# Attention spread evenly over the MLP, and a third MLP pair by seven products, on one Trainium2 core

## The chip, the cores and the metric

The kernel runs on one core of one Trainium2 chip. A time is the device time of one execution in microseconds, and a kernel's time is the median of several executions. A profile is one execution taken by the hardware profiler. The engines are named as the profile names them: PE (TensorE matmuls), PEld (TensorE weight loads), DVE (VectorE), ACT (ScalarE), POOL (GpSimd) and SP (SyncE, which here only issues DMAs).

## The reference

There are 8 batches, 12 heads, 448 positions, 64 values a head, so a model width of 768, and a hidden width of 3072. All inputs and the output are float32.

```python
q_n, k_n = rmsnorm(q, g_q), rmsnorm(k, g_k)            # over the 64 values of a head
attn = softmax(q_n @ k_n.T / sqrt(64))                  # 448 x 448, per batch and head
x    = heads_side_by_side(attn @ v)                     # (8, 448, 768)
h    = x.transpose(0, 2, 1) @ U @ V                     # mixes positions, rank 32
u    = x + h.transpose(0, 2, 1)
out  = u + relu(u @ w_ch1) @ w_ch2                      # 768 -> 3072 -> 768
```

## The kernel before

The 8 x 448 positions are cut into 28 tiles of 128 rows; two batches make seven tiles, so that the middle tile of seven holds the end of one batch and the start of the next. The kernel has two kinds of work. Attention makes x for one batch at a time; the MLP takes u in tiles. After a hand-written head (batch 0's attention), the MLP runs as a chain of generators: the first three tiles, a single tile, and then twelve pairs of tiles, `mlp_pair(g)` for g = 1 to 12 with tiles 2g+2 and 2g+3. Each `yield` in a generator is a step of some six matmuls. All engines take their instructions in the order in which the program issues them (`tc.manual_schedule`), and no scheduler moves them.

**A pair.** `mlp_pair` has two layers, called ph and po here after their PSUM tiles. In the first layer of an ordinary pair (L638 to L652), each of 24 blocks of hidden values takes 6 matmuls of 256 columns (L643), 144 in all, and one relu serves two blocks (L428 on ACT, L430 on DVE). The second layer uses a Strassen-Winograd form: 7 products of 12 matmuls of 384 columns, 84 in all (L519), with sums of weights (T1 to T4) and of hidden values (S1 to S4, L527). The products are called W, Z, X and Y by their banks; W, X and Y get two products each, Z one. DVE adds x (L674, L677, L696), and the rest goes through `part` (L686, L699, L711); POOL does two of the additions (L687, L702). At the end of it `put` stores the two tiles.

**A late pair.** From pair `LATE` = 11 on, the first layer goes through `products_late`, the same scheme for `w_ch1`: 7 products of 36 matmuls of 128 columns (L592), 252 in all, in an order written out as "10 50 11 20 ..." (product, then third of the hidden width). Three groups (72, 32 and 42) are held back into the second layer. It needs four sums of weights with 12 pieces each, R1, R2, R4 and R3, where R3 takes the place of V21 inside `w1b`, and four sums of u (`sums_u`). Copies on ACT (L602, L604) and additions on DVE (L606, L608) carry partial results between PSUM and two buffers, `held`, which live in the buffers E of attention. In the first late pair alone, two dummy matmuls (L601) write two banks once.

**Queues within the program.** `later` puts small sums into `pending`, `spread` puts the sums of weights into `slack`. Each `step` first issues one of `pending` or, if there is none, one of `slack`; then it lets the MLP take a step. A late pair first empties `slack`.

**Weaving.** `weave(fill, upto, items)` spreads the pieces of a batch's attention (or of its mixing, `mixing`) evenly over MLP steps up to a place. `attention(b)` makes pairs of heads p = 6b to 6b+5: scores (L303), exps (L311), value products (L318) and their normalization (L333 to L347) into x; along the way squares (L235), reductions (L240), `rsqrt` (L245, L246), scalings (L255) and gains (L290) for pairs of heads two to four ahead, and their loads. Where three scores come in one session, one of them uses two banks of the pool "mm" (tile `sh`), which the MLP and the value products use too: it has four. R1 is put into `slack` at pair of heads 44, R2 and R4 at 46, into buffers that attention has just done with. The places where attention ends:

```python
ends = {2: ("po", 1), 3: ("po", 3), 4: ("ph", 5), 5: ("po", 6), 6: ("po", 8), 7: ("po", 10)}
for b, key in ends.items():
    weave(fill, place(key, 0.05), attention(b))
    weave(fill, place(key, 0.6), mixing(b))
```

Counted in stages (a stage is a pair, its first layer the first 0.533 of it), attention 2 ends at 1.557, 3 at 3.557, 4 at 5.027, 5 at 6.557, 6 at 8.557 and 7 at 10.557, each mixing some 0.257 later.

**Rings.** x has NX = 9 places, u has 4. `have_read` tells that a pair has read its u, and issues the transposes on SP that waited for the place (`turn_u`, L405). With nine places some normalizations of three tiles wrap around the ring and are split into two instructions (L342). `sums` and `rms` have six slots of 16, by pair of heads.

Of the kernel before, what the change touches and what calls it, by code (L numbers as in the profile page):

```python
# [10 lines left out]
FP32 = mybir.dt.float32  # L11
BF16 = mybir.dt.bfloat16
# [6 lines left out]
def kernel(  # L19
# [74 lines left out]
    one = consts.tile([1, 1], FP32, name="one")  # L94
    eps = consts.tile([SP, 1], FP32, name="eps")
    rk0 = consts.tile([SP, 8], FP32, name="rk0")
    sums = consts.tile([SP, 6 * 16], FP32, name="sums")
    NE, NV, NQ, NWARM = 2, 3, 4, 12
    Ew = [consts.tile([P, 2, PAD + NJ * S + PAD], BF16, name=f"E{i}") for i in range(NE)]
    Es = [e[0:SP] for e in Ew]  # L100
    vw = [consts.tile([P, HG, NJ, D + 1], BF16, name=f"va{i}") for i in range(NV)]
    vas = [v[0:SP] for v in vw]


    NX, NU = 9, 4
    xr = consts.tile([P, NX, dm], BF16, name="xr")
    ur = consts.tile([P, KD, NU * P], BF16, name="ur")
    zero = xr[:, NX - 1]
# [2 lines left out]
    vL = consts.tile([P, HG, NJ * D], FP32, name="vt")  # L111
    part = consts.tile([P, HALF], FP32, name="part")

    rms = consts.tile([SP, 6 * 16], FP32, name="rms")
    banks0 = []

    def rs_of(p, n=1, of=None):

        c = 16 * (p % 6)
        return (of or (banks0[3][0:SP] if p < 8 and p not in (2,) else rms))[:, c:c + 16 * n]  # L120

    def as_v(x):
# [9 lines left out]
    def setup():  # L132
        nc.vector.memset(zero, 0.0)
        nc.gpsimd.memset(eps, D * 1e-6)
        nc.gpsimd.memset(one, 1.0)
        for i, g in enumerate((g_q, g_k)):
            nc.gpsimd.dma_start(grow[:, i], bass.AP(g.tensor, g.offset, [[0, 1], [0, 2], [1, D]]))
        nc.gpsimd.memset(shift, 0.0)
        make_identity(nc, ident)
        for t in Es:  # L140
            nc.gpsimd.memset(t[:, :, 0:PAD], 0.0)
            nc.gpsimd.memset(t[:, :, PAD + NJ * S:], 0.0)
        for t in vas:
            nc.gpsimd.memset(t[:, :, :, D:D + 1], 1.0)
        for t in qkTs:
            nc.gpsimd.memset(t[:, SQK:], 0.0)
        nc.gpsimd.memset(Vsh, 0.0)
# [157 lines left out]
            scs[p, kc] = sc  # L305

    def expo(p, kc):
        E, sc = Es[p % NE][:, :, PAD + kc * S:PAD + (kc + 1) * S], scs.pop((p, kc))
        parts = [(E, sc[2][0:SP, :, 0:S])] if len(sc) > 2 else [(E[:, h], sc[h][0:SP, 0:S]) for h in range(2)]
        for dst, src in parts:  # L310
            nc.scalar.activation(dst, src, AF.Exp, scale=float(D) ** 0.5)  # L311

    def products(p, hh, o):
        par, E, va, hl = p // 6 % 2, Es[p % NE], vas[(p // 2) % NV], 2 * (p % 2) + hh
        for i, off in enumerate(OFFS[par]):
            for kc in range(NJ):
                c = PAD + kc * S + off
                nc.tensor.matmul(o[:, i, :], E[:, hh, c:c + P], va[:, hl, kc, :],  # L318
                                 start=(kc == 0), stop=(kc == NJ - 1))

    def tiles_of(b):
# [85 lines left out]
    def have_read(ts):  # L407
        read.update(ts)
        for t in [t for t in waiting if t - NU in read]:
            waiting.remove(t)  # L410
            turn_u(t)
# [14 lines left out]
    def relu(out, ph, on_act):  # L426
        if on_act:
            nc.scalar.activation(out, ph, AF.Relu)  # L428
        else:
            nc.vector.tensor_relu(out, ph)  # L430
# [5 lines left out]
    def put(t, osb, cols=slice(0, dm), engines=(nc.sync, nc.sync)):  # L436
        b, off = where(t)
        if off < 0:
            store(b - 1, 384, 448, osb, 0, cols, engines)
            store(b, 0, 64, osb, 64, cols, engines)  # L440
        else:
            store(b, off, off + P, osb, 0, cols, engines)
# [83 lines left out]
    def later(fn, *args):  # L526
        pending.append(lambda: fn(*args))  # L527

    LATE = 11
    wq = w1b.rearrange("p (d i) (k j n) -> p j d k i n", d=2, j=2, n=P)  # L530
    Q = KH // 2
    V11, V12, V21, V22 = ([wq[:, j, d, k] for k in range(Q)] for j in range(2) for d in range(2))
    R1, R2, R4 = [], [], []
    R3 = V21
    tq = Ew[0][:, 0, 0:4 * KD // 2 * P].rearrange("p (c i n) -> p c i n", c=4, n=P)
    flat = Ew[1].rearrange("p a n -> p (a n)")
    held = [x.bitcast(FP32) for x in (Ew[0][:, 1, 0:1024], flat[:, 0:1024], flat[:, 1024:2048], flat[:, 2048:3072])]

    def pieces(tile_, names, dtype=FP32):
        x = tile_.rearrange(names)  # L540
# [30 lines left out]
    def products_late(g, u):  # L571
        b11, b21, b22 = quarter(u, 0, 0), quarter(u, 1, 0), quarter(u, 1, 1)
        t1, t2, t3, t4 = (tq[:, c] for c in range(4))
        sides = {1: (V11, b11), 2: (V12, b21), 3: (R4, b22), 4: (V22, t4), 5: (R1, t1), 6: (R2, t2), 7: (R3, t3)}
        Pb, Zb, Qb = {}, {}, {}

        def bank(tag):
            if tag == "s":
                return ps_s.tile([P, 2, 512], FP32, tag="s", name="sc")[:, 0]
            return ps_mm.tile([P, 512], FP32, tag="mm", name="ph")  # L580

        def one(m, n):
            ks = slice(4 * n, 4 * n + 4)
            left, right = sides[m]
            if m == 1:
                Pb[n] = bank("mm")
            elif m == 5:
                Zb[n] = bank("mm")
            to = {1: Pb, 2: Pb, 5: Zb, 3: Zb}.get(m, Qb)[n]
            for j in range(4):  # L590
                for i in range(KD // 2):
                    nc.tensor.matmul(to[:, j * P:(j + 1) * P], left[4 * n + j][:, i], right[:, i],  # L592
                                     start=m in (1, 5) and j == 0 and i == 0, stop=i == KD // 2 - 1,
                                     skip_group_check=True)
                if j % 2:
                    yield 2 * P
            keep, tmp = held[n % 2], held[2 + n % 2]
            if m == 1:
                Qb[n] = bank("s")
                if g == LATE and n < 2:  # L600
                    nc.tensor.matmul(Qb[n], w1b[:, 0, 0:P], w1b[:, 0, 0:512], start=True, stop=True)  # L601
                nc.scalar.copy(Qb[n], Pb[n])  # L602
            elif m == 5:
                nc.scalar.copy(keep, Zb[n])  # L604
            elif m == 6:
                nc.vector.tensor_tensor(Zb[n], Qb[n], keep, OP.add)  # L606
            elif m == 7:
                nc.vector.tensor_tensor(tmp, Qb[n], keep, OP.add)  # L608
                relu(hB[:, 3, ks].rearrange("p k n -> p (k n)"), tmp, True)
            elif m == 2:  # L610
                relu(hB[:, 0, ks].rearrange("p k n -> p (k n)"), Pb.pop(n), True)
            elif m == 3:
                relu(hB[:, 1, ks].rearrange("p k n -> p (k n)"), Zb.pop(n), False)
            else:
                relu(hB[:, 2, ks].rearrange("p k n -> p (k n)"), Qb.pop(n), True)
                sums_h(n)

        def run(order):
            for word in order.split():
                yield from one(int(word[0]), int(word[1]))  # L620

        yield from run("10 50 11 20 60 51 21 70 30 61 40 12 52 71 31 22 62 41")
        return run("72 32"), run("42")
# [7 lines left out]
    def mlp_pair(g):  # L631
        t0, u, last = 2 * g + 2, u_of(2 * g + 2, 2), 2 * g + 4 == 28
        left = None
        if g >= LATE:
            while slack:
                slack.pop(0)()
            left = yield from products_late(g, u)
        for k in range(KH // 2 if g < LATE else 0):  # L638
# [13 lines left out]
            yield 2 * P  # L652
        if g == LATE - 1:
            spread(nc.vector.tensor_tensor, R3, V11, V21, OP.subtract)
        have_read([t0, t0 + 1])
        x0, x1 = x_of(t0), x_of(t0 + 1)
        c0, c1 = slice(0, HALF), slice(HALF, dm)
        osb0, osb1 = new_osb(), new_osb()
# [5 lines left out]
        for n in product(W, A11, B11, True):  # L664
            yield n
            if left:
                yield from left[0]
        nc.scalar.copy(part, W)
        yield HALF
        if left:  # L670
# [26 lines left out]
            yield c.stop - c.start  # L697
        yield from product(X, S3, T3, False)
        nc.vector.tensor_tensor(part, X, part, OP.add)  # L699
        if not last:  # L700
            both = osb1.rearrange("p (h n) -> p h n", h=2)
            nc.gpsimd.tensor_tensor(both, both, part.rearrange("p n -> p () n").to_broadcast([P, 2, HALF]), OP.add)  # L702
            put(t0 + 1, osb1)
# [102 lines left out]
    def step(fill):  # L806
        if pending:
            pending.pop(0)()
        elif slack:
            slack.pop(0)()  # L810
        n = next(fill, None)
        if n is not None:
            at[0] += n
        return n

    def weave(fill, upto, items):
        weights, total = sum(w for w, _ in items), upto - at[0]
        done = due = 0.0
        for w, piece in items:
            due += w * total / max(weights, 1)  # L820
            while done < due:
                n = step(fill)
                if n is None:
                    break
                done += n
            piece()
# [163 lines left out]
    with tc.manual_schedule():  # L990
# [32 lines left out]
        def place(key, share):  # L1023
            return begins[key][0] + share * begins[key][1]
# [24 lines left out]
        load(8)  # L1049
        while at[0] < place("single", 0):  # L1050
            step(fill)
        ends = {2: ("po", 1), 3: ("po", 3), 4: ("ph", 5), 5: ("po", 6), 6: ("po", 8), 7: ("po", 10)}
        for b, key in ends.items():
            weave(fill, place(key, 0.05), attention(b))
            weave(fill, place(key, 0.6), mixing(b))
        while step(fill) is not None:
            pass

# [29 lines left out]
```

## Time and profile before

| | us |
|---|---|
| median of 3 runs | 563.0 (562.41 to 564.17) |
| the profiled execution | 561.54 |
| its span, first to last instruction | 559.8 |
| pairs 1 to 10, from 122.1 to 497.7 | 36.3 to 40.6 each |
| pair 11 (497.7 to 527.5) | 29.8 |
| pair 12 with the end (527.5 to 559.8) | 32.3 |

The profiled execution's time is 1.7 us more than its span, for what lies around the first and last instruction. The granted TensorE clock is 1.00 in the whole span. A row of the profile's waits reads "engine tile line <- releaser: us in total, times, longest". In the chain, a piece is its start, its length and what ran. Busy times of matmuls overlap each other, so that a rate is read from the steps of the chain and not from the mean of a row.

### The profile page before, as it was taken

What the parts mean: (1) busy time and instruction counts of PE and PEld (TensorE: products, weight loads), DVE (VectorE), ACT (ScalarE), POOL (GpSimd) and SP (SyncE); (2) the same over time, 40 slices, a digit from 0 to 9 for tenths busy, and PEclk for the clock granted to TensorE, in tenths of its full rate; (3) what the DMA queues carried; (4) which work ended last, traced back from release to release, by engine and by line L of the source; (5) the groups of instructions that cost most, each with busy time, mean ns of one, the idle gap of its engine ahead of it and who ended that gap; (6) DMA issues with size and microseconds to landing.
All of it is one profiled execution on the core that took longest, in us unless ns stands there. A gap on an engine that the chain in (4) does not pass through costs nothing.

```text
span 559.8 us, 13728 instructions
## 1 busy us (share of the span) xinstructions
PE 549.7 (98%) x5688; PEld 387.3 (69%) x5690; DVE 366.0 (65%) x827; ACT 316.7 (57%) x536; POOL 177.7 (32%) x174
## 2 busy tenths in 40 slices
PE   8999999999999999999999999999999999989996
PEld 3665565767768677586785785776867758768785
DVE  6977867498655656656566677465464585785554
ACT  7967640778357574487548780765717746315150
POOL 6964026444051340344404440433205320010200
PEclk9999999999999999999999999999999999999999
DMA  8999996945555551365347565635605121040101
GB/s 287 292 235 239 204 251 182 201 144 160 130 112 135 146 141 64 75 186 147 90 142 160 134 145 116 155 85 153 170 16 126 42 19 59 2 114 1 52 7 56
DMA packets 108445, 72.41 MB, mean 129 GB/s; under 512 B 56688, under 2 KB 105056, under 8 KB 108384
## 3 DMA queue, kind: packets, MB, share of 16 engines
q1 hardware_dynamic: 96800, 61.65, 43.8%
q0 software_dynamic: 11008, 9.44, 10.4%
q8 instruction: 44, 0.72, 0.5%
q10 hardware_dynamic: 576, 0.46, 0.3%
q14 instruction: 17, 0.14, 0.1%
HBM read 56.78 MB, written 11.01 MB: 121 GB/s over the span
## 4 chain that ended last, share of the span: by engine, by line
PE 91%; ACT 5%; DVE 3%; issue 1%
PE po L519 30%; PE ph L643 28%; PE o L318 8%; PE sc L303 4%; PE po L474 4%; PE ph L456 3%; ACT E L311 3%; PE ph L592 3%; PE sh L303 3%; PE sc L592 2%; PE px L395 1%; PE sc L830 1%; DVE comb L515 1%; PE ph L484 1%; PE sc L843 1%
## 5 line engine op out<-in xcount | busy, mean ns | idle before, releaser
L643 PE MATMUL ph<-ur,w1b 128*128 128x256 bf16 x1440 | 170.9, 273 | 0.0
L643 PEld LDWEIGHTS <-w1b 128*128 128x128 bf16 x1440 | 135.7, 98 | 26.2 <-issue 10.0
L519 PEld LDWEIGHTS <-hT 128*128 128x128 bf16 x1032 | 96.2, 98 | 64.7 <-issue 7.7
L311 ACT ACTIVATE E<-sc 112x896 bf16<-112x896 f32 x138 | 121.8, 918 | 2.1 <-PE sc L303 2.1
L255 POOL TENSOR_TENSOR qkn<-qk,rms 112x512 bf16<-112x512 f32 (+1 forms) x73 | 80.8, 1127 | 109.0 <-ACT rms L246 96.4
L519 PE MATMUL po<-w2b,hT 128*128 128x384 bf16 (+1 forms) x588 | 103.8, 323 | 0.2 <-ACT hT L428 0.2
L311 ACT ACTIVATE E<-sh 112x448 bf16<-112x448 f32 x108 | 52.9, 541 | 90.1 <-PE sh L303 90.1
L428 ACT ACTIVATE hT<-ph 128x512 bf16<-128x512 f32 (+1 forms) x110 | 64.3, 587 | 52.1 <-PE ph L643 45.0
L527 DVE TENSOR_TENSOR hT<-hT 128x512 bf16<-128x512 bf16 x144 | 71.6, 508 | 12.9 <-ACT hT L428 10.8
L519 PE MATMUL po<-comb,hT 128*128 128x384 bf16 (+1 forms) x444 | 78.3, 322 | 0.0
L687 POOL TENSOR_TENSOR osb<-osb,xr 128x384 f32<-128x384 f32 x12 | 12.8, 1071 | 187.5 <-DVE osb L686 181.2
L318 PEld LDWEIGHTS <-E 112*128 112x128 bf16 x1536 | 60.7, 98 | 8.8 <-issue 2.8
L318 PE MATMUL o<-va,E 112*128 112x65 bf16 x1344 | 57.1, 194 | 0.1
L333 DVE RECIPROCAL rec<-o 128x4 f32<-128x4 f32 x84 | 15.0, 179 | 55.3 <-PE o L318 54.9
L430 DVE TENSOR_SCALAR hT<-ph 128x512 bf16<-128x512 f32 (+1 forms) x48 | 31.8, 662 | 29.3 <-PE ph L643 27.0
L240 DVE TENSOR_REDUCE sums<-sq 112x16 f32<-112x1024 f32 x32 | 38.7, 1210 | 6.4 <-ACT sq L235 6.3
L303 PE MATMUL sc<-qkT 64*128 64x448 bf16 x268 | 38.9, 351 | 1.0 <-ACT E L311 0.6
L474 PE MATMUL po<-w2b,hT 128*128 128x384 bf16 x192 | 34.5, 326 | 0.1
L235 ACT ACTIVATE sq<-qk 112x1024 f32<-112x1024 f32 x32 | 33.8, 1056 | 0.0
L342 DVE TENSOR_TENSOR xr<-o,rec 128x192 bf16<-128x192 f32 (+1 forms) x108 | 31.5, 310 | 2.9
L397 DVE TENSOR_TENSOR xr<-px,xr 128x384 bf16<-128x384 f32 x56 | 29.5, 549 | 5.4 <-PE px L393 2.9
L303 PEld LDWEIGHTS <-qkT 64*128 64x128 bf16 x376 | 14.3, 94 | 25.6 <-issue 15.8
(153 smaller groups left out, 566.0 us busy)
## 6 DMA issues: line engine op xcount, KB each, us to landing
qk<-in_q_dram SPq DMA_DIRECT2D x44, 256.0 KB, 4.3
qk<-in_k_dram SPq DMA_DIRECT2D x44, 256.0 KB, 4.9
vt<-in_v_dram SPq DMA_DIRECT2D x17, 512.0 KB, 6.2
w1b<-in_moe_w_ch_dram POOLq DMA_DIRECT2D x6, 768.0 KB, 19.5
w2b<-in_moe_w_ch_dram POOLq DMA_DIRECT2D x6, 768.0 KB, 36.5
comb<-in_v_dram SPq DMA_DIRECT2D x5, 512.0 KB, 8.8
out_dram<-osb SPq DMA_DIRECT2D x7, 336.0 KB, 3.2
out_dram<-osb SPq DMA_DIRECT2D x7, 288.0 KB, 3.1
```

The costliest lines, as they stand in the source:

```text
L235: nc.scalar.activation(dst, src, AF.Square)
L240: nc.vector.tensor_reduce(rs_of(p, of=sums).rearrange("p (s h j) -> p s h j", s=2, h=2)[:, :, hs], sqs[p].rearrange("p (s h j d) -> p s h ...
L255: (nc.gpsimd if p >= 12 or pool else nc.vector).tensor_tensor(out[:, g], x[:, g], rs[:, g].to_broadcast([SP, g.stop - g.start, NJ, D]), OP ...
L303: nc.tensor.matmul(sc[hh][0:n, 0:S], flat[pp, c:c + n], blocks(p)[pp, :, 0], start=True, stop=True)
L311: nc.scalar.activation(dst, src, AF.Exp, scale=float(D) ** 0.5)
L318: nc.tensor.matmul(o[:, i, :], E[:, hh, c:c + P], va[:, hl, kc, :], start=(kc == 0), stop=(kc == NJ - 1))
L428: nc.scalar.activation(out, ph, AF.Relu)
L430: nc.vector.tensor_relu(out, ph)
L474: nc.tensor.matmul(po, left(hc), w2b[:, half, hc, :], start=(hc == 0), stop=(hc == KH - 1))
L519: nc.tensor.matmul(bank, left[:, k, :], right[:, k, cols], start=start and k == 0, stop=k == KH // 2 - 1, skip_group_check=not start)
L527: pending.append(lambda: fn(*args))
L643: nc.tensor.matmul(out, w1b[:, dc, hc * P:(hc + 1) * P], u[:, dc, :], start=(dc == 0), stop=(dc == KD - 1))
```

## The change

- `LATE` becomes 10, so the first layer of pair 10 goes through seven products too. `have_read` of a late pair comes after the groups that are held back, since they read u.
- Attention of batch b ends at stage 1.557 + 1.6 (b - 2), its mixing 0.257 later: 1.557, 3.157, 4.757, 6.357, 7.957 and 9.557.
- A step without `pending` issues two of `slack`. A late pair first issues all of `pending`, then `slack` down to the 12 sums of R3; each group of product 7 issues the R3 that it reads, if they are still there.
- In pairs 9, 10 and 11 DVE makes the last two additions to `osb1` (two instructions) in place of POOL (one).
- x has 10 places; `sums` and `rms` have four slots. The two halves of E share the padding between them. `held` is two buffers, and product 7 adds in place.

```diff
-    sums = consts.tile([SP, 6 * 16], FP32, name="sums")
+    sums = consts.tile([SP, 4 * 16], FP32, name="sums")
...
-    Ew = [consts.tile([P, 2, PAD + NJ * S + PAD], BF16, name=f"E{i}") for i in range(NE)]
+    ROW = NJ * S + PAD
+    Ew = [consts.tile([P, PAD + 2 * ROW], BF16, name=f"E{i}") for i in range(NE)]
...
-    NX, NU = 9, 4
+    NX, NU = 10, 4
...
-        c = 16 * (p % 6)
+        c = 16 * (p % 4)
...
-    LATE = 11
+    LATE = 10
...
-    held = [x.bitcast(FP32) for x in (Ew[0][:, 1, 0:1024], flat[:, 0:1024], flat[:, 1024:2048], flat[:, 2048:3072])]
+    held = [Ew[1][:, i * 1024:(i + 1) * 1024].bitcast(FP32) for i in range(2)]
...
+            while m == 7 and len(slack) > Q - 4 * (n + 1):
+                slack.pop(0)()
...
-                nc.vector.tensor_tensor(tmp, Qb[n], keep, OP.add)
-                relu(hB[:, 3, ks].rearrange("p k n -> p (k n)"), tmp, True)
+                nc.vector.tensor_tensor(keep, Qb[n], keep, OP.add)
+                relu(hB[:, 3, ks].rearrange("p k n -> p (k n)"), keep, True)
...
         if g >= LATE:
-            while slack:
+            while pending:
+                pending.pop(0)()
+            while len(slack) > Q:
                 slack.pop(0)()
...
-        have_read([t0, t0 + 1])
+        if not left:
+            have_read([t0, t0 + 1])
...
             if left:
                 yield from left[0]
+                have_read([t0, t0 + 1])
...
-        if not last:
+        if LATE - 1 <= g and not last:
+            for h in (c0, c1):
+                nc.vector.tensor_tensor(osb1[:, h], osb1[:, h], part, OP.add)
+            put(t0 + 1, osb1)
+        elif not last:
...
     def step(fill):
         if pending:
             pending.pop(0)()
-        elif slack:
-            slack.pop(0)()
+        else:
+            for _ in slack[:2]:
+                slack.pop(0)()
...
-        ends = {2: ("po", 1), 3: ("po", 3), 4: ("ph", 5), 5: ("po", 6), 6: ("po", 8), 7: ("po", 10)}
-        for b, key in ends.items():
-            weave(fill, place(key, 0.05), attention(b))
-            weave(fill, place(key, 0.6), mixing(b))
+        def stage(x):
+            g = int(x)
+            return begins["ph", g][0] + (x - g) * (begins["ph", g + 1][0] - begins["ph", g][0])
+
+        for b in range(2, B):
+            end = 1.557 + 1.6 * (b - 2)
+            weave(fill, stage(end), attention(b))
+            weave(fill, stage(end + 0.257), mixing(b))
```

More of the change, by code (lines that the diff above doesn't have):

```diff
@@ L112 @@
     part = consts.tile([P, HALF], FP32, name="part")
-    rms = consts.tile([SP, 6 * 16], FP32, name="rms")
+    rms = consts.tile([SP, 4 * 16], FP32, name="rms")
     banks0 = []
     def rs_of(p, n=1, of=None):
-        c = 16 * (p % 6)
+        c = 16 * (p % 4)
         return (of or (banks0[3][0:SP] if p < 8 and p not in (2,) else rms))[:, c:c + 16 * n]
@@ L140, in setup @@
         for t in Es:
-            nc.gpsimd.memset(t[:, :, 0:PAD], 0.0)
-            nc.gpsimd.memset(t[:, :, PAD + NJ * S:], 0.0)
+            nc.gpsimd.memset(t[:, 0:PAD], 0.0)
+            nc.gpsimd.memset(t[:, PAD:].rearrange("p (h n) -> p h n", h=2)[:, :, NJ * S:], 0.0)
         for t in vas:
@@ L307, in expo @@
     def expo(p, kc):
-        E, sc = Es[p % NE][:, :, PAD + kc * S:PAD + (kc + 1) * S], scs.pop((p, kc))
+        E = Es[p % NE][:, PAD:].rearrange("p (h n) -> p h n", h=2)[:, :, kc * S:(kc + 1) * S]
+        sc = scs.pop((p, kc))
         parts = [(E, sc[2][0:SP, :, 0:S])] if len(sc) > 2 else [(E[:, h], sc[h][0:SP, 0:S]) for h in range(2)]
@@ L316, in products @@
             for kc in range(NJ):
-                c = PAD + kc * S + off
-                nc.tensor.matmul(o[:, i, :], E[:, hh, c:c + P], va[:, hl, kc, :],
+                c = PAD + hh * ROW + kc * S + off
+                nc.tensor.matmul(o[:, i, :], E[:, c:c + P], va[:, hl, kc, :],
                                  start=(kc == 0), stop=(kc == NJ - 1))
@@ L534 @@
     R3 = V21
-    tq = Ew[0][:, 0, 0:4 * KD // 2 * P].rearrange("p (c i n) -> p c i n", c=4, n=P)
-    flat = Ew[1].rearrange("p a n -> p (a n)")
-    held = [x.bitcast(FP32) for x in (Ew[0][:, 1, 0:1024], flat[:, 0:1024], flat[:, 1024:2048], flat[:, 2048:3072])]
+    tq = Ew[0][:, 0:4 * KD // 2 * P].rearrange("p (c i n) -> p c i n", c=4, n=P)
+    held = [Ew[1][:, i * 1024:(i + 1) * 1024].bitcast(FP32) for i in range(2)]
     def pieces(tile_, names, dtype=FP32):
@@ L596, in one @@
                     yield 2 * P
-            keep, tmp = held[n % 2], held[2 + n % 2]
+            keep = held[n % 2]
             if m == 1:
```

## The prediction, as it was put on record

> **What bounds the kernel now.** I read the page first: engine shares, then the chain that ended last, then what TensorE waited for, the chain in order of time and the stretches by stage.
>
> ```profile
> PE 549.7 (98%) x5688; PEld 387.3 (69%) x5690; DVE 366.0 (65%) x827; ACT 316.7 (57%) x536; POOL 177.7 (32%) x174
> ...
> PE 91%; ACT 5%; DVE 3%; issue 1%
> ```
>
> TensorE is the bound: 91% of the chain, and it is busy in 98% of the span. Since a busy matmul row may still be waiting, I looked at what TensorE waited for by name (in total, times, longest):
>
> ```profile
> PE sc L601 <- DVE w1b L547: 1.5, 1, 1.5
> PE sc L830 <- DVE xr L133: 1.3, 1, 1.3
> PE sh L303 <- ACT hT L428: 1.0, 2, 0.6
> PE sc L303 <- ACT E L311: 0.6, 2, 0.4
> PE sc L303 <- DVE qkT L274: 0.3, 1, 0.3
> PE po L519 <- ACT hT L428: 0.2, 1, 0.2
> ```
>
> Five of these six lie before 145 us, where the change moves nothing on TensorE, or at 500 us (L601). Between 145 and 497 us the one wait is the last row, 0.23 us at 295.5 us. So there are two things to win: matmul columns, and the wait at L601. The pieces of the chain that price them (start us, us, what), from an ordinary pair's first layer and from the seven-product one:
>
> ```profile
> 404.34 3.93 PE ph L643 x36
> ...
> 497.88 0.68 PE ph L592 x12
> 498.57 0.04 issue
> 498.61 0.55 DVE osb L711
> 499.15 0.27 DVE qkn L547
> 499.42 0.55 DVE w1b L547 x2
> 499.96 0.04 issue
> 500.01 0.38 PE sc L601
> 500.38 1.34 PE ph L592 x24
> ```
>
> A 256-column step takes 3.93/36 = 109.2 ns, a 128-column one 1.34/24 = 55.8 ns, and the chain leaves TensorE for VectorE just once late in the kernel, at 498.6 us.
>
> **A third pair by seven products.** Pair 10's first layer was 144 x 109.2 ns = 15.72 us. It becomes 7 x 36 = 252 matmuls x 55.8 ns = 14.06 us. The gain is 1.66 us of pure TensorE time. The trace holds the result already: pair 12 runs its first 216 late matmuls in 12.0 us (527.5 to 539.5), at 55.6 ns, with no wait. The two 512-column dummies (L601) only move from pair 11 to pair 10. ScalarE gets 6 copies and loses 3 relus, VectorE gets 3 relus, 6 additions of 0.69 us and 4 sums of u: ScalarE was busy 7.1 of 12.0 us and VectorE 6.1 in that stage of pair 12, so TensorE hides them.
>
> [...]
>
> **The weight sums.** In the old order the 12 sums R3 come last in VectorE's queue and the first L601 reads two of them, so TensorE stood from 498.34 to 500.01 us, 1.67 us for a 0.05 us step: 1.62 us. Ahead of them stood one sum of 1.98 us where its neighbours start 0.27 us apart:
>
> ```profile
> 496.66 1.81 POOL L702 TENSOR_TENSOR osb<-osb,part 128x768 f32<-128x768 f32 x1 [3.50 <-DVE part L699]
> 496.71 1.98 DVE L547 TENSOR_TENSOR qkn<-w1b,qkn 128x384 bf16<-128x384 bf16 x1
> ```
>
> This is GpSimd's addition at L702 holding VectorE up. In pairs 9 to 11 it becomes two VectorE additions (0.55 us each by L707): 1.1 us more work, but GpSimd has only L687 left there.
>
> In the new order R1 (12 sums) is issued in pair 8's second layer, R2 and R4 (24) in pair 9's first, and six of R3 among the first 30 matmuls of pair 9's second; the first L601 then finds its two R3 long done and waits for nothing. What is late next? Behind product X, VectorE has part (0.56), two additions (1.10), one sum of u (0.35), two R3 (0.54) and L711 (0.55), 3.1 us in all. From X's end TensorE has 12 x 0.163 = 1.95 us of Y, then 48 narrow matmuls, 2.7 us, before the group that needs L711's bank: 4.6 us of cover. So the 1.62 us goes, and VectorE may be 1.5 us late before anything comes back.
>
> Is VectorE that late? Counted in the order of the changed program, each instruction at its row's mean, it has in pair 9 19.0 us beside some 20.2 us of TensorE in the first layer and 18.4 beside 16.1 in the second; for pair 10 before, the same count gives 16.1 and 20.7, of which the trace shows 11.6 and 14.1 us busy, because neighbouring instructions overlap, and TensorE waited nowhere ahead of L601. New is that two sums a step are popped: up to ten in 3.3 us of TensorE, 10 x 0.27 = 2.7 us where GpSimd is idle, which fits. I take zero; the bounds are 0 (a wait cannot be negative) and the whole 1.62 us.
>
> **Attention at even distances.** Matmul count and work are the same; only the places move. Batch 3 shrinks from 1.74 stages to 1.34, batches 6 and 7 likewise; batches 4 and 5 stretch from 1.21 and 1.27 to 1.34. The old wait of 0.23 us sits at batch 5's start and goes with it. New waits come if ScalarE falls behind: by the same count, the new first layer of pair 7 holds 21.0 us of ScalarE beside 20.3 of TensorE, those of pairs 2, 4 and 5 19.2 to 19.5. But pair 4 before held 22.2 beside 21.4, without a wait.
>
> ```profile
> core 0: us, PE busy (x) PEld busy (x) DVE busy (x) ACT busy (x) POOL busy (x), PEclk, DMA share, GB/s
> 122.10:145.40 23.30, 23.08 (x280) 18.24 (x279) 19.53 (x48) 19.64 (x33) 11.07 (x8) 1.00 0.64 142
> 235.30:257.30 22.00, 22.00 (x265) 17.62 (x263) 13.48 (x29) 19.44 (x33) 11.54 (x11) 1.00 0.59 151
> 352.40:372.00 19.60, 19.60 (x212) 15.99 (x210) 9.68 (x21) 14.96 (x26) 6.20 (x7) 1.00 0.55 145
> ```
>
> These are the first layers of pairs 1, 4 and 7: with a dense batch ScalarE is busy 19.4 to 19.6 us and TensorE still full. The price of the dense batches of before is 0 (batch 4) and 0.23 us (batch 5), 0.12 in the mean; five such batches cost 0.6 us. The far end is batch 2, the densest, which paid the 1.0 us of the row "PE sh L303 <- ACT hT L428": 5.0 us for five. I take 0.6, as batches 4 and 5 are the nearer in density (1.21 and 1.27 against 1.34). The loads, transposes and scalings of a batch move with it on SP's and GpSimd's queues; in the stretch of pair 4 the DMA engines were 0.59 busy and GpSimd 11.5 us of 22, and no wait on either reached TensorE: zero.
>
> **The rest.** The tenth place of x saves 12 split normalizations on VectorE (about 0.15 us each), off the path. Four slots for sums and rms instead of six: a slot's last reader is an engine's work two pairs of heads earlier, some 16 us. A shared pad in E and two held buffers instead of four change no instruction's size; the order of the seven products leaves several groups between two uses of a buffer. Transposes of u for tiles 26 and 27 go out on SP's queue in pair 10's second layer rather than right after the first; they have over a stage (30 us) before pair 12, against 3 us each. All zero.
>
> **Sum** against the profiled execution, 561.54 us (span 559.8): -1.66 - 1.62 - 0.23 + 0.60 = -2.91, so 558.6. That execution lies 1.5 us under the median of 563.0 of the three runs; the same difference from the median gives 560.1.
>
> **Rivals.**
> *VectorE late at pair 10.* If the sums pile up, for instance one again behind GpSimd's L687 (a sum beside it took 1.07 us at 455.7), the wait at the late pair's start returns in another place, with up to 1.62 us; with 0.6 us more of ScalarE waits it is 562.3, no change. For it: the 18.4 us beside 16.1. Against it: 4.6 us of cover for 3.1 of work.
>
> *ScalarE on the path, slower.* At a batch's start its queue puts two exps, the two instructions of rsqrt, a gain and a square, 4.1 us at 291.3 to 295.0, ahead of the next relu; TensorE went on for 36 matmuls (3.9 us) and then waited 0.23 us. In the new order the batches 4, 5 and 7 start inside a first layer. Were its banks used up after 12 matmuls (1.31 us), each start would cost 2.8 us, 8.4 in all: -3.51 + 8.4, so 567.9. It decides for slower by over 1.7 us once the cover is under 2.4 us, some 22 matmuls. Against it: the trace's cover is 36, and ScalarE was never the name of a longer wait behind 145 us.
>
> *The narrow products don't save.* If loads were not hidden, 252 x 98 ns (the row of L592's weight loads) = 24.7 us, 9.0 more than before: 563.0 + 9.0 - 1.62 - 0.23 + 0.6 = 570.7. Against it: pair 12's 12.0 us. [...]
>
> **How the numbers follow.** Forecast 0.76, VectorE late 0.13, ScalarE 0.08, narrow products 0.03. 0.3% (1.7 us) is about what a measurement can tell from no change: faster is under 561.3, slower over 564.7. The forecast is faster unless new waits pass 1.8 us, which takes 0.05 of it to "same"; of the VectorE case 0.03 stays faster. So 0.74 faster, 0.15 same, 0.11 slower. The range begins at no new wait at all, 559.5, less 0.6 for the runs' own spread (562.41 to 563.0), 558.9; it ends at the VectorE case with the same spread, 562.9. The ends above it are the 0.11.
>
> **What would show it.** Pair 10's first layer with 216 narrow matmuls in about 12.5 us (the dummies included) and no "L601 <- DVE" row; pair 9's second layer without a TensorE wait on VectorE; waits of ScalarE's relus or exps on TensorE between 145 and 450 us of 0.3 to 1 us in sum. The prediction is wrong if those pass 1.8 us, if the narrow step at pair 10 is over 60 ns, or if the granted clock falls under 1.00.

## The result, and the profile after

The changed kernel takes 559.34 us (559.03 to 560.66, median of six executions), the kernel before 562.42 us (561.93 to 564.17, six): ratio 0.9946, interval 0.9929 to 0.9962. The gain is 3.1 us, where the forecast had 2.9 and 560.1 us; of the 0.8 us between 560.1 and the median, 0.6 is the start, since the kernel before has a median of 562.42 over six executions and had 563.0 over three. The profiled execution is 559.42 us, its span 557.6.

Over the fourteen profiles of this study the start of the single tile lies anywhere from 100.1 to 102.1 us, with nearly the same work ahead of it, while what lies behind it repeated within 0.05 us where the changed kernel was profiled twice (457.02 and 457.06 us). So I compare kernels from that start to the end, "behind the head" below: before 459.69 us, after 457.02, so 2.67 us less. This isn't free of the head either: in twelve profiles pair 1 starts 22.01 to 22.06 us behind the single tile, in two others 22.27 and 22.67, after a wait of TensorE for the gain L291 at 113 or 114 us, which itself waited for a transpose. Where it matters, the difference from pair 1 on is given too.

From the page of the changed kernel, busy time by engine and the chain's shares:

```profile
PE 547.9 (98%) x5796; PEld 387.4 (69%) x5798; DVE 375.3 (67%) x834; ACT 318.1 (57%) x539; POOL 174.0 (31%) x171
...
PE 88%; DVE 5%; ACT 3%; issue 1%; DMA 1%; SPq 1%; POOL 0%; DVEq 0%; POOLq 0%
```

TensorE has 108 more matmuls (252 - 144) and 1.8 us less busy time; it is still the bound. What TensorE waited for in the changed kernel (in total, times, longest):

```profile
PE sc L842 <- DVE xr L134: 1.3, 1, 1.3
PE sh L304 <- ACT hT L430: 1.0, 2, 0.6
PE sc L304 <- DVE qkT L275: 0.6, 1, 0.6
PE sc L304 <- ACT E L313: 0.6, 2, 0.4
...
PE o L320 <- DVE hT L432: 0.2, 1, 0.2
```

The row of L601 (now L604) and the 0.23 us of batch 5's start are gone; the last row, at 412.4 us, is one of four new waits. It is a relu L432 that stands on VectorE behind three sums of hidden values, which take 2.98 us beside GpSimd, where one takes some 0.42 us by itself:

```profile
409.17 2.98 DVE L529 TENSOR_TENSOR hT<-hT 128x512 bf16<-128x512 bf16 x3 [3.24 <-ACT hT L430]
409.46 2.40 POOL L256 TENSOR_TENSOR qkn<-qk,rms 112x512 bf16<-112x512 f32 x2
412.07 0.68 DVE L432 TENSOR_SCALAR hT<-ph 128x512 bf16<-128x512 f32 x1
```

The chain where the late pairs now begin, in order of time:

```profile
465.95 3.74 PE po L521 x23
469.69 0.67 PE ph L595 x12
470.36 0.05 issue
470.41 1.50 PE ph L595 x24
471.91 0.22 PE sc L604
472.13 0.67 PE ph L595 x12
```

The chain stays on TensorE past both dummies. They cost 0.2 us each and no wait. Stretches of the changed kernel, of which the first is pair 9's second layer and the others are the first 216 late matmuls of pairs 10 and 11:

```profile
core 0: us, PE busy (x) PEld busy (x) DVE busy (x) ACT busy (x) POOL busy (x), PEclk, DMA share, GB/s
453.00:469.50 16.50, 16.43 (x122) 9.69 (x119) 14.50 (x39) 0.72 (x2) 0.91 (x1) 1.00 0.11 25
469.50:482.00 12.50, 12.45 (x219) 12.24 (x218) 7.83 (x18) 7.10 (x12) 0.00 (x0) 1.00 0.22 66
497.70:509.70 12.00, 12.00 (x217) 12.00 (x216) 6.24 (x12) 7.10 (x12) 0.00 (x0) 1.00 0.22 68
```

Pair 10 runs its narrow matmuls at pair 11's rate, 12.0/216 = 55.6 ns, plus two dummies. VectorE is busy 14.5 of 16.5 us ahead of it: close to full, and TensorE waits there once, 0.23 us at 464.1 us for the addition L399 of VectorE.

### The profile page after: what moved, and what is told of

Read it like the earlier page. It is cut to its first block, busy times and chain, and to the rows that moved or that the text cites. A ratio compares the mean times of both kernels' runs of the same rounds, so it can differ in the third digit from the quotient of the medians.

```text
span 557.6 us, 13969 instructions
## 1 busy us (share of the span) xinstructions
PE 547.9 (98%) x5796; PEld 387.4 (69%) x5798; DVE 375.3 (67%) x834; ACT 318.1 (57%) x539; POOL 174.0 (31%) x171
## 4 chain that ended last, share of the span: by engine, by line
PE 88%; DVE 5%; ACT 3%; issue 1%; DMA 1%; SPq 1%; POOL 0%; DVEq 0%; POOLq 0%
PE po L521 28%; PE ph L648 24%; PE o L320 8%; PE po L476 5%; PE sc L304 4%; PE ph L595 4%; PE ph L458 3%; PE sc L595 3%; PE sh L304 3%; ACT E L313 2%; PE px L397 1%; DMA qk<-in_k_dram 1%; PE ph L486 1%; DVE hT L529 1%; PE bank L320 1%
## 5 line engine op out<-in xcount | busy, mean ns | idle before, releaser
L648 PE MATMUL ph<-ur,w1b 128*128 128x256 bf16 x1296 | 156.0, 273 | 0.0
L648 PEld LDWEIGHTS <-w1b 128*128 128x128 bf16 x1296 | 121.8, 98 | 25.9 <-issue 10.8
L256 POOL TENSOR_TENSOR qkn<-qk,rms 112x512 bf16<-112x512 f32 (+1 forms) x73 | 83.0, 1157 | 152.4 <-ACT rms L247 111.5
L313 ACT ACTIVATE E<-sc 112x896 bf16<-112x896 f32 x138 | 122.0, 920 | 2.2 <-PE sc L304 2.1
L430 ACT ACTIVATE hT<-ph 128x512 bf16<-128x512 f32 (+1 forms) x101 | 58.9, 586 | 71.1 <-PE ph L648 63.8
L529 DVE TENSOR_TENSOR hT<-hT 128x512 bf16<-128x512 bf16 x144 | 73.2, 527 | 17.3 <-ACT hT L430 15.4
L313 ACT ACTIVATE E<-sh 112x448 bf16<-112x448 f32 x108 | 52.9, 543 | 55.9 <-PE sh L304 55.8
L320 PEld LDWEIGHTS <-E 112*128 112x128 bf16 x1536 | 60.7, 98 | 10.2 <-issue 2.9
L432 DVE TENSOR_SCALAR hT<-ph 128x512 bf16<-128x512 f32 (+1 forms) x51 | 33.8, 663 | 19.6 <-PE ph L648 17.2
L399 DVE TENSOR_TENSOR xr<-px,xr 128x384 bf16<-128x384 f32 x56 | 29.9, 551 | 8.1 <-PE px L397 5.1
L236 ACT ACTIVATE sq<-qk 112x1024 f32<-112x1024 f32 x32 | 33.9, 1059 | 0.0
L344 DVE TENSOR_TENSOR xr<-o,rec 128x192 bf16<-128x192 f32 (+1 forms) x96 | 30.8, 331 | 2.9
```

The costliest lines, as they stand in the source:

```text
L236: nc.scalar.activation(dst, src, AF.Square)
L256: (nc.gpsimd if p >= 12 or pool else nc.vector).tensor_tensor(out[:, g], x[:, g], rs[:, g].to_broadcast([SP, g.stop - g.start, NJ, D]), OP ...
L320: nc.tensor.matmul(o[:, i, :], E[:, c:c + P], va[:, hl, kc, :], start=(kc == 0), stop=(kc == NJ - 1))
L648: nc.tensor.matmul(out, w1b[:, dc, hc * P:(hc + 1) * P], u[:, dc, :], start=(dc == 0), stop=(dc == KD - 1))
```

## The experiments

Ratios are to the kernel before, run on the same chip. Line numbers are the changed kernel's, except in the first experiment.

**The wait at L601 by itself.** In the kernel before, the dummies read weights that no sum overwrites:

```diff
-  nc.tensor.matmul(Qb[n], w1b[:, 0, 0:P], w1b[:, 0, 0:512], start=True, stop=True)
+  nc.tensor.matmul(Qb[n], w1b[:, 3, 0:P], w1b[:, 3, 0:512], start=True, stop=True)
```

> The kernel before, in which the two dummy matmuls L601 read rows of w1b that the sums R3 don't write (w1b[:, 3] in place of w1b[:, 0]); their values are not used. Theory: the whole wait of 1.62 us at 498.3 us hangs on these two sums, so the first late pair starts without it and nothing else is late: before - 1.6, some 560.8 us, and 'PE sc L601 <- DVE w1b L547' is gone from the waits. Rival (VectorE is late anyway): the wait moves to the group that needs L711's bank or the one that reads R3, and the time stays within 0.5 us of before.

Measured 561.12 us, ratio 0.9987 (0.9968 to 1.0007), which alone doesn't tell it from no change (one of twelve executions took 567.30 us; the medians are 1.2 us apart). Behind the head it is 1.16 us less (458.53), and the row of L601 is gone. The rest of the 1.62 us is in the timeline of this kernel (start, length, engine, line, operation):

```profile
499.51 3.30 DVE L547 TENSOR_TENSOR w1b<-w1b 128x384 bf16<-128x384 bf16 x12
502.73 0.68 DVE L606 TENSOR_TENSOR ph<-sc,E 128x512 f32<-128x512 f32 x1
503.47 0.83 PE L592 MATMUL sc<-E,w1b 128*128 128x128 bf16 x12 [0.30 <-DVE ph L606]
```

The twelve sums of R3 still stand in one piece on VectorE, and the addition L606 behind them is now what TensorE waits for (its step is 0.47 us over its columns). Removing only the wait is worth 1.2 us; issuing the sums earlier gets the rest.

**Without the third pair.**

```diff
-    LATE = 10
+    LATE = 11
```

> The changed kernel with LATE = 11 again: two pairs by seven products, all else as changed. Theory: the third pair is worth its columns, 1.66 us, so some 561.0 us, with pair 10's first layer (144 matmuls) in 15.7 us without attention in it and pair 11's (216) in 12.5 with the dummies. Rival (the third pair saves nothing, the gain comes from the removed wait and the spread of attention): equal to the changed kernel, 559.3.

Measured 561.42 us, ratio 0.9990 (0.9981 to 0.9999). Pairs 10 and 11 together take 57.52 us (29.37 + 28.15) against 55.87 (28.15 + 27.72): 1.65 us, where the count of columns gave 1.66. Behind the head the difference is 1.75, but 0.26 of it is the wait at 114 us just named. From pair 1 on it is 1.49, because without the third pair the wait at 464.1 us in pair 9 is gone too (pair 9 takes 37.47 us instead of 37.63).

**Uneven distances, up to batch 6 at 1.14 to 1.40 stages.**

```diff
-            end = 1.557 + 1.6 * (b - 2)
+            end = (1.557, 3.557, 5.027, 6.557, 7.957, 9.557)[b - 2]
```

> The changed kernel with attention's ends at 1.557, 3.557, 5.027, 6.557, 7.957 and 9.557: batches 3 to 5 as before, batch 6 in 1.14 stages, batch 7 as changed. Theory: even spacing itself is worth little; batch 6, denser than any before, adds 0.2 to 1.0 us of waits of TensorE on ScalarE: 559.5 to 560.4. Rival (even spacing is where the gain lies): 1.5 us or more slower than the changed kernel, 561 and up.

Measured 559.81 us, ratio 0.9961 (0.9949 to 0.9972); 0.35 us more behind the head. The dense batch 6 pays one wait of 0.7 us at 357.8 us, for a gain of L291 on ScalarE:

```profile
357.98 0.67 ACT L291 ACTIVATE qkT<-qkT,gg 128x448 bf16<-128x448 bf16 x1 [1.35 <-DMA qkT<-qkn]
```

ScalarE isn't the bound here, though I had expected it: it sat idle for 1.35 us until the transpose that the gain reads had landed. GpSimd's scaling L256, behind its addition L713, had let that transpose start only at 355.04 us. The even distances themselves matter little.

**The last addition of pairs 9 to 11 back on GpSimd.**

```diff
-        if LATE - 1 <= g and not last:
+        if False:
```

> The changed kernel with the addition of part to osb1 on GpSimd again in pairs 9 to 11 (L702 of before). Theory: one sum R3 stands behind it for 1.98 us as before, L711 comes about 1.2 us later, and both lie under the 4.6 us of cover: equal to the changed kernel, 559.3 to 559.7. Rival (GpSimd's hold of VectorE was what put the wait on the path): 1 to 1.7 us slower, with a wait of TensorE on L711 at pair 10's start.

Measured 559.69 us, ratio 0.9958 (0.9946 to 0.9970); behind the head 0.07 us more. This part of the change is worth nothing that these runs can tell.

**One weight sum a step.**

```diff
-            for _ in slack[:2]:
+            for _ in slack[:1]:
```

> The changed kernel with one weight sum a step again in place of two. Theory: with 1.34 stages for batch 7 the steps left are too few, so VectorE enters pair 10 with a dozen or so sums in its queue (0.27 us each), and what the old order lost at the first late pair comes back in part: 0.5 to 1.7 us slower than the changed kernel, 559.8 to 561.1, as a wait of TensorE on VectorE at pair 10's start. Rival (the rate does not matter, the cover of 4.6 us holds): equal to the changed kernel, 559.3, no such wait.

Measured 562.97 us, ratio 1.0008 (0.9994 to 1.0022), and 3.81 us more behind the head. So all of the gain is lost, over twice what I expected. TensorE's wait in this kernel and two stretches around it:

```profile
PE sc L604 <- DVE w1b L548: 2.5, 1, 2.5
```

```profile
core 0: us, PE busy (x) PEld busy (x) DVE busy (x) ACT busy (x) POOL busy (x), PEclk, DMA share, GB/s
469.00:472.00 3.00, 0.50 (x10) 0.38 (x7) 3.00 (x12) 0.00 (x0) 0.00 (x0) 1.00 0.74 224
472.00:476.00 4.00, 3.76 (x37) 3.59 (x38) 2.11 (x8) 1.73 (x3) 0.00 (x0) 0.59 0.10 35
```

The first dummy stands behind the backlog of sums, 2.7 us over its columns. What I had missed is in the second row: the granted clock falls. It is 0.5 for 3.41 us from 472.73 (twelve late matmuls take 1.49 us there, at 474.75, and 0.67 at 478.26), which adds half of that, 1.7 us, where TensorE has work throughout. The two make 4.4 us; pair 10 takes 4.31 us more, and pair 9 takes 0.58 us less (37.05 instead of 37.63), since two of the changed kernel's new waits, at 434.0 and 464.1 us, are gone. So two sums a step have a price of their own in pair 9. Of the twelve executions, the five at a mean clock of 1.000 have a median of 561.48 us and the seven at 0.996 to 0.997 one of 563.25: the same 1.8 us apart.

So a wait of 2.51 us (2.7 over its columns) came with the lower clock in seven of twelve executions. What sets the other five apart is not shown.

**One sum a step, and dummies that don't read the sums.** The edit above and that of the first experiment.

> One sum a step, as in e5, and the dummies read rows that R3 doesn't write, as in e1. Theory: e5 lost 2.7 us to the wait of the dummies for R3 and some 1.7 us to the clock of 0.5 that this wait brought about; without it TensorE goes on, waits in pieces of under 1 us for sums later in VectorE's queue, and the granted clock stays 1.00: 0.5 to 1.2 us slower than the changed kernel. Rival (VectorE's backlog costs the same wherever TensorE meets it): 3 us or more slower, as e5.

Measured 560.13 us, ratio 0.9964 (0.9952 to 0.9976); only 0.45 us more than the changed kernel behind the head. One wait is left:

```profile
PE sc L595 <- DVE ph L609: 0.8, 1, 0.8
```

The clock stays at 1.00. Pair 10 loses 0.98 us to that wait, and pair 9 again takes 0.58 us less. So VectorE's lateness itself costs one microsecond at pair 10, half a microsecond in all. It was dear only where TensorE met all of it at one instruction, with 2.7 us over its columns and 1.7 us more at the clock of 0.5.

**Nine places for x.** With nine, x is partly overwritten before the MLP has read it, so some rows of the output aren't the reference's; all else is unchanged.

```diff
-    NX, NU = 10, 4
+    NX, NU = 9, 4
```

> The changed kernel with nine places for x. Theory: the split normalizations come back on VectorE, and with them the wait of 0.30 us in batch 2 (at 122.8 us before, absent after); elsewhere nothing: 0.3 us slower than the changed kernel. Rival (the place is needed for the even spacing): waits of TensorE of over 1 us in batches 5 to 7, where x would wait for tiles that the MLP still reads.

Measured 560.54 us, ratio 0.9969 (0.9957 to 0.9981); 0.71 us more behind the head, of which 0.48 in the stage of pair 1, where a wait at batch 2 comes back that the kernel before also had (122.8 us): the second of two score matmuls that otherwise start 4 ns apart comes 0.48 us after the first. The tenth place isn't free of effect, as I had taken it to be.

**Narrow dummies.** They write only the last 64 of the bank's 512 columns, and some of the output isn't the reference's: a price, not a version to use.

```diff
-  nc.tensor.matmul(Qb[n], w1b[:, 0, 0:P], w1b[:, 0, 0:512], start=True, stop=True)
+  nc.tensor.matmul(Qb[n][:, S:512], w1b[:, 0, 0:P], w1b[:, 0, S:512], start=True, stop=True)
```

> The changed kernel with the two dummy matmuls 64 columns wide (the 64 that attention's scores never write) in place of 512. Theory: pair 10's first layer takes the time of the later ones, 0.35 to 0.4 us less; under what the medians can tell (558.9 to 559.3), but seen in the stage. Rival: the dummies lie beside something else and nothing changes.

Measured 559.59 us, ratio 0.9953 (0.9941 to 0.9965). Pair 10 takes 27.78 us instead of 28.15: the dummies cost 0.37 us and no more. Behind the head it is 0.35 us more, with 0.66 in the wait at 113 us, which this edit doesn't reach; from pair 1 on it is 0.32 less.

**Denser batches, at 1.4 stages.**

```diff
-            end = 1.557 + 1.6 * (b - 2)
+            end = 1.557 + 1.4 * (b - 2)
```

> The changed kernel with attention's ends 1.4 stages apart in place of 1.6 (1.14 stages of attention for each of batches 3 to 7). Part of the computation is changed: batch 6 writes over a tile of x that the MLP still needs, so the output of some rows is not the reference's; the work is the same. Theory (ScalarE has room at 1.34 stages and little at 1.14): some 0.3 to 0.7 us of waits on ScalarE for each of the five batches, as batch 6 of the uneven run had 0.68, so 1 to 3 us slower than the changed kernel. Rival (ScalarE is no bound at this density either): within 0.5 us of the changed kernel.

Measured 569.31 us, ratio 1.0130 (1.0117 to 1.0143); 10.2 us more behind the head, far above what I expected. The two longest of TensorE's waits:

```profile
PE o L320 <- DVE osb L722: 3.4, 1, 3.4
PE po L521 <- ACT hT L430: 1.8, 1, 1.8
```

The second, at 386 us, is the prediction's ScalarE rival: exps, a gain and a square of a batch's start (L313, L291, L236) stand ahead of one relu. It is real at 1.4 stages, at one batch start, and leaves the clock at 1.00. The first, at 406.6 us, isn't ScalarE: four sums of R1 take 4.7 us on VectorE beside GpSimd's work, and L722 stands behind them. From 409.2 us the clock is 0.5 for 6.83 us, in 5.76 of which TensorE has work, so another 2.9 us. The two waits (3.55 and 1.92 us over their columns) and the clock make 8.4 of the 10.2; the rest is in several waits of 0.2 to 0.9.

**At 1.5 stages, and at 1.62.** The same line with 1.5, then with 1.62.

> Attention's ends 1.5 stages apart (1.24 stages of attention a batch). Part of the computation is changed, as at 1.4: a tile of x is overwritten early. Theory: batches 4 and 5 of before had 1.21 and 1.27 stages and cost 0 and 0.3 us, so this density costs some 0.5 to 1.5 us over the changed kernel for five batches. Rival (the loss at 1.4 sets in gradually): 5 us slower, half of what 1.4 lost.

> Attention's ends 1.62 stages apart, so that batch 7 ends at 9.657 and its mixing at 9.914. Theory: the remaining 0.9 us of waits move about with the places; within 0.5 us of the changed kernel, unless the sums that follow batch 7 come late for pair 10, which would cost 0.5 to 2 us. Rival (1.6 is the tightest that works, more room is better): 0.5 us faster or more.

1.5 stages: 566.11 us, ratio 1.0067 (1.0055 to 1.0079), 5.7 us more behind the head. 1.62 stages: 564.59 us, ratio 1.0043 (1.0028 to 1.0057), 4.7 us more behind the head. For both, the theory that the price of density is small and gradual missed; 1.62 is even less dense than 1.6 and had been expected to cost nothing. R1's sums (L548) in the changed kernel, at 1.6:

```profile
428.52 1.15 DVE L548 TENSOR_TENSOR qk<-w1b 128x384 bf16<-128x384 bf16 x4
430.06 2.23 DVE L548 TENSOR_TENSOR va<-w1b 128x384 bf16<-128x384 bf16 x2
430.22 1.85 POOL L713 TENSOR_TENSOR osb<-osb,part 128x768 f32<-128x768 f32 x1 [2.69 <-DVE part L706]
433.05 0.56 DVE L722 TENSOR_TENSOR osb<-po,osb 128x384 f32<-128x384 f32 x1
```

and at 1.62:

```profile
430.77 4.46 DVE L548 TENSOR_TENSOR qk<-w1b 128x384 bf16<-128x384 bf16 x4
430.94 1.85 POOL L713 TENSOR_TENSOR osb<-osb,part 128x768 f32<-128x768 f32 x1 [2.39 <-DVE part L706]
432.75 2.27 POOL L256 TENSOR_TENSOR qkn<-qk,rms 112x512 bf16<-112x512 f32 x2
435.16 0.54 DVE L722 TENSOR_TENSOR osb<-po,osb 128x384 f32<-128x384 f32 x1
435.75 0.67 PE L320 MATMUL o<-va,E 112*128 112x65 bf16 x16 [3.37 <-DVE osb L722]
```

At 1.6 R1 begins at 420.38 us; its seventh to tenth sums take 1.15 us ahead of GpSimd's L713, only the last two stand beside it, and L722 starts at 433.05. At 1.62, where batch 7 lies 0.1 stages further on, R1 begins at 423.66, and its seventh to tenth sums stand beside L713 and then L256: 4.46 us. L722 starts 2.1 us later, and TensorE, which needs its bank, idles 3.37 us. The clock is 0.5 for 3.41 us from 436.87, so 1.7 us more: 3.4 + 1.7 = 5.1 covers the 4.7. One execution whose clock stayed at 1.000 took 562.29 us, the three at 0.997, of which the profile is one, 563.4 to 564.3, and the four at 0.992 to 0.994 564.9 to 566.3.

At 1.5 stages it is the same engine pair in pair 8's first layer:

```profile
412.34 2.16 POOL L256 TENSOR_TENSOR qkn<-qk,rms 112x512 bf16<-112x512 f32 x2 [7.93 <-ACT rms L247]
412.50 2.21 DVE L548 TENSOR_TENSOR qk<-w1b 128x384 bf16<-128x384 bf16 x2
```

The normalizations of x (L344, L348) come behind such sums and behind a sum of hidden values (L529, 1.26 us beside L256); TensorE's scores wait 1.76 us for L348, and again the clock is 0.5 for 3.41 us, from 419.68. That wait (the matmul comes 2.1 us late) and the clock make 3.8 of the 5.7 us; the remainder is in many waits under 1 us.

Alone, four sums take 1.15 us; beside GpSimd one takes some 1.1 us (4.46/4). What holds them up there is not shown. A kernel with R1 moved to another place at the same distances was not run, so these rows show the longer sums in three kernels but not their removal.

**The changed kernel once more**, on the same chip as those two.

> The changed kernel again, on the same chip as the others: 3 us under the kernel before, with the same waits of TensorE behind the head as in its first profile.

559.70 us (559.01 to 560.15), ratio 0.9955 (0.9942 to 0.9968), and the same waits. No usable kernel of the study beat it.

## Why the prediction was right, and where it wasn't

| term, us | forecast | measured | from |
|---|---|---|---|
| third pair | -1.66 | -1.65 | pairs 10 and 11, with and without it |
| wait at L601 | -1.62 | -1.62 | its row gone, nothing in its place |
| wait at 295 us | -0.23 | -0.30 | the step against like steps |
| new waits | +0.60 | +1.14 | four steps at 223.5 (0.16), 412.4 (0.33), 434.0 (0.42) and 464.1 us (0.23) |
| tenth place | 0 | -0.48 | pair 1's stage, 39.84 us before and with nine places, 39.36 after |
| sum | -2.91 | -2.91 | |
| behind the head | | -2.67 | |

That the two sums are equal is chance: the new waits were mis-sized by about as much as the tenth place was left out. The 0.24 us between the last two lines lie in steps too short to name. From pair 1 on the score matmuls take 30.75 us start to start instead of 30.70, where the terms above would make it some 0.4 less, which would hold it, but no run tests that.

**Third pair.** Right in mechanism and size: pairs 10 and 11 show 55.6 ns a narrow matmul, and in pair 12 a group of twelve takes 0.67 us.

**The wait at L601.** Right, and the cover was real: VectorE was nearly as full in pair 9's second layer as allowed for (14.5 of 16.5 us), and nothing came back at pair 10. Two sums a step is the part that carries it: with one a step VectorE is late at this very place, and the kernel loses 3.8 us with the clock (0.45 if the dummies read other weights). But the zero that I took for them wasn't zero: two of the new waits, in pair 9, go when one sum a step is issued, and pair 9 is 0.58 us shorter. The two additions on VectorE, which I costed at nothing, cost or bring nothing.

**New waits.** The size was low by half, and the mechanism was mostly wrong. Only 0.16 us, at 223.5 us, is the wait on ScalarE that was forecast. 0.33 is a relu on VectorE behind sums beside GpSimd (412.4 us), and the two in pair 9 are additions and normalizations of VectorE (L399, L348) that come late where two sums a step are issued.

**The steps that failed** are the zero for two sums a step, above, and "the change moves nothing on TensorE" before 145 us, with "off the path" for the tenth place. With ten places a wait in pair 1 goes, with nine it is there; that the split normalizations saved on VectorE are the reason is argued, not shown. That its 0.48 us offsets the low price of the new waits is luck.

**The rivals.** I priced "VectorE late" at pair 10 with 1.62 us at most. The mechanism, a sum beside GpSimd, exists (four take 4.46 us there, 1.15 alone), but it strikes at R1 in pair 8, which I had not priced, and costs 4.7 us at 1.62 stages, since the granted clock, which I had taken to stay at 1.00, follows with 0.5 for 3.41 us. ScalarE on the path takes a denser batch than 1.6 stages, and the one dense batch among uneven ones waited for a transpose instead. The forecast came out within a margin that I didn't know of: 0.02 stages more a batch, by which R1 starts 3.3 us later, make the kernel slower than before. Neither the queue counts nor the cover at L601 showed that.

## What to carry to other kernels

When small VectorE instructions are moved, look at what GpSimd does in the stretch they land in, and at who waits behind them on VectorE; a place that fits by counts can lie 3 us from one that costs 5 us, so run the neighbouring placements too. Price a new TensorE wait with the clock it may cost as well (here waits of 2.51 and 3.37 us were each followed by 3.41 us at 0.5), and break a backlog into several short waits rather than let one instruction meet all of it. To compare kernels at a few tenths of a per cent, measure from a landmark behind a head that varies from run to run, and look at single stages too: here a stage just behind the landmark still varied by 0.7 us.

## What the runs showed of the hardware

- After a wait of 2.51 us in a TensorE stream that is otherwise full (one sum a step) the granted clock was 0.5 for 3.41 us in the profiled execution; seven of twelve executions had a mean clock of 0.996 to 0.997, five 1.000. At 1.62 stages it was 0.5 for 3.41 us after a wait of 3.37 us, at 1.4 stages for 6.83 us after one of 3.4 us. At 1.5 stages TensorE's idle time of 1.76 us at 417 us was followed by 3.41 us at 0.5 too, but at 1.4 stages 1.75 us at 386 us was not, nor were the 1.5 us of the kernel before.
- In the 3.41 us (the length of most of the stretches at 0.5) just ahead of these falls TensorE was busy 0.90 us (one sum a step), 1.10 (1.4 stages), 1.11 (1.62) and 1.66 (1.5). In 3.41 us that hold a whole wait without a fall it was busy 1.66 us at most (1.4 stages, 386 us) and 1.96 (before, 497.70 to 501.11 us). What decides whether the clock falls is not shown.
- Four bf16 sums of 128 x 384 took 1.15 us on VectorE alone (changed kernel, 428.52 us) and 4.46 us beside GpSimd (1.62 stages, 430.77 us).
